# Another written-out order for the first thousand operations of an attention, MoE and bilinear kernel on one core

## The chip, the core and the metric

The kernel runs on one core of a Trainium2 chip. The core has four compute engines with a queue of instructions each: TensorE (PE in the profile; PEld is its weight load), VectorE (DVE), ScalarE (ACT) and GpSimd (POOL); SyncE (SP) issues most DMAs. Each engine works its own queue strictly in program order; between engines an instruction waits on semaphores. SBUF holds the tiles, PSUM the matmul results in banks of 128 partitions by 2 KB. The metric is the device time of one execution in microseconds (us), as the median of several runs.

## The reference

```python
scores = scale * q @ k^T                     # B 2, H 8, S 576, D 64
bias = -(cum[:, :, :, None] - cum[:, :, None, :])   # cum: running sum of max(s, 0)
scores = np.where(causal, -1e9, scores + np.minimum(bias, 0.0))
attn = softmax(scores); x = (attn @ v)       # x: 1152 x 512
logits = x @ w_gate; P = exp(logits - max)   # 8 experts, then 8 rounds of Sinkhorn
for e in range(E):
    h = np.maximum(x @ w1[e], 0.0)           # 512 -> 1024
    out += P[:, e:e+1] * (h @ w2[e])         # 1024 -> 512
a = x @ w_a; b = x @ w_b                     # x is out now; 512 -> 1536
return (a * b) @ w_out                       # 1536 -> 512
```

## The kernel before, in words

Every large product is made of three fp16 matmuls. Each fp32 operand is scaled by a power of two and split into a high and a low half; high times high, high times low and low times high are summed in PSUM. The power of two comes from the largest magnitude of the whole tensor, so before a weight can be used it has to be loaded, its squares' maxima taken (`w_prep`, L483; ACT at L521), reduced over a row (DVE, L451), reduced over the partitions, turned into a power of two (`pow2`, L257), and applied: ACT writes the high half (L296), DVE the low half (L310). The reduction over partitions is `all_max` (L472): a PE transpose (L477) into columns 320 to 456 of one of two PSUM banks, `xp0` and `xp1`, a DVE reduction (L478), and a PE matmul with ones (L479) that spreads the result. Those two banks are also where attention collects its output (L1161). `scales` (L620) does the same for q and k: L642 to L647, the matmuls L688 and L690, and a chain of small DVE steps, L653 to L674. `augs` (L697 to L706) uses its result for extra columns of k, which `k_prep` (L730) transposes by DMA (L753) into the tile `ka2`; q goes the same way through `q_prep` (L759).

The work is tiled by 128 tokens: 9 tiles, of which tile 8, the tail of both batches, is 64 rows of each. Tiles 0 and 4, the first of each batch, have only one block of keys and are done apart in fp32 (`first_tile`, L1093): transposes (L1125), scores (L1137), DVE maximum and subtraction (L1145, L1146), exponent on ACT (L1149), transpose (L1153), product with v (L1161). `x_tile` (L1168) normalizes a tile's output, transposes it (L1192) and splits it into `xt` (L1197 on ACT, L1199 on DVE). For the other tiles, `row_max` (L786; matmuls L799, mask L784, DVE L803), `shift` (L838; L846 to L848, PE L853) and `probs` (L862; scores L893 and L894, exponent L903, product with v L936 to L938) follow. The tail tile goes another way, `row_path` (L955), with 64-row matmuls at L998 and L1017.

The experts begin as soon as a tile of x and a unit of weights are there: `h_quad` (L1280) computes four blocks of 128 hidden units for 128 tokens into one PSUM bank, `mb0` or `mb1`, each as 12 matmuls of 128 columns (L1293 to L1295); ACT's Relu (L1299) and DVE (L1300) split it. I call 12 of these "12 h". `y_part` (L1304) multiplies by w2 (L1313 to L1315, 512 columns).

What sets the order: `Graph.add` collects every operation with its engine, its cost and the keys that it reads and writes. `schedule` then lays them out. For the operations before `cut` (1023 of them, up to the second expert) the order is written out in the table `ORDER`, whose entries are four times the operation's number plus the choice of engine; what lies behind the cut is laid out by a greedy list scheduler that starts from the times at which the table leaves the engines. `emit` (L165) issues the operations in that one sequence, so each engine's queue is the sequence's part for that engine. A dependency is tracked by the tile framework for whole tiles: a matmul into a PSUM bank waits for earlier readers of any column of that bank.

## Time and profile before

| | |
|---|---|
| median of 3 runs | 1007.16 us (1007.16 to 1007.33) |
| the profiled execution | 1006.66 us |
| its span, first to last instruction | 1004.9 us |
| PE busy | 986.5 us, 98% of the span |
| DVE busy | 784.2 us, 78% |
| ACT busy | 550.8 us, 55% |
| POOL busy | 101.1 us, 10% |
| granted PE clock | 1.00 by the page, in every stretch |

Times in the text are those of the profiled execution, counted from the start of its span. A row of the timeline gives the start, the duration of one piece (or of a run of like pieces, with their count), the engine, the line, the operation, what it writes and reads, and, if the engine stood idle before it, how long and what ended that. Matmuls are pipelined, so a matmul's duration is longer than its distance to the next one; the distance is what it costs.

### The profile page before, as it was taken

Reading aid. Unit: us, or ns where it says so; the run is one execution under the profiler, and the core shown is the slowest. Engines: PE = TensorE matmul, PEld = TensorE weight load, DVE = VectorE, ACT = ScalarE, POOL = GpSimd, SP = SyncE. Lnnn points to the kernel's source line nnn. Section 1 sums busy time; section 2 is a strip of 40 time slices with the busy share of each in tenths; the row PEclk is TensorE's granted clock in tenths of the full one; section 3 lists DMA queues with packets and bytes.
Section 4 is the critical chain, followed back from the end, with each engine's and each line's share of the span. In section 5 each row is a group of like instructions: output and inputs, shape, how many; then the busy total and the mean of one; then the engine's idle time right before and its main releaser. Section 6 shows DMA issues by size and latency. Waiting matters only on the chain.

```text
span 1004.9 us, 19286 instructions
## 1 busy us (share of the span) xinstructions
PE 986.5 (98%) x7714; PEld 636.3 (63%) x7714; DVE 784.2 (78%) x1688; ACT 550.8 (55%) x1062; POOL 101.1 (10%) x152
## 2 busy tenths in 40 slices
PE   6799999999999999999999999999999999999998
PEld 5677767776467447646744764674476464455777
DVE  4899986798867998885799888579988988676502
ACT  5898755457477347726634772663464455455220
POOL 3364554000000000000000000000000000000000
PEclk9999999999999999999999999999999999999999
DMA  9986999122133263233326323322636432322202
GB/s 232 212 163 126 172 160 173 34 84 85 45 104 105 84 220 133 77 113 109 105 84 224 132 75 114 107 105 84 226 138 253 108 84 84 126 85 85 84 22 74
DMA packets 152011, 121.40 MB, mean 121 GB/s; under 512 B 113361, under 2 KB 127697, under 8 KB 147313
## 3 DMA queue, kind: packets, MB, share of 16 engines
q1 hardware_dynamic: 147008, 117.78, 41.8%
q10 hardware_dynamic: 4912, 2.40, 1.0%
q8 instruction: 60, 0.98, 0.4%
q14 instruction: 31, 0.25, 0.1%
HBM read 79.26 MB, written 21.23 MB: 100 GB/s over the span
## 4 chain that ended last, share of the span: by engine, by line
PE 93%; DVE 3%; DMA 2%; ACT 1%; issue 1%; POOL 1%; ACTq 0%; DVEq 0%; POOLq 0%
PE yb L1313 10%; PE yb L1315 10%; PE yb L1314 10%; PE yb L1753 5%; PE yb L1755 5%; PE yb L1754 5%; PE mb L1753 4%; PE mb L1755 4%; PE mb L1754 4%; PE yb L2201 2%; PE yb L2200 2%; PE yb L2199 2%; PE mb L1313 2%; PE mb L1315 2%; PE mb L1314 2%; PE mb L2201 2%
## 5 line engine op out<-in xcount | busy, mean ns | idle before, releaser
L1315 PE MATMUL yb<-wun,ht 128*128 128x512 f16 x480 | 181.9, 379 | 0.0
L1314 PE MATMUL yb<-wun,ht 128*128 128x512 f16 x480 | 181.9, 379 | 0.0
L1313 PE MATMUL yb<-wun,ht 128*128 128x512 f16 x480 | 181.9, 379 | 0.0
L1315 PEld LDWEIGHTS <-ht 128*128 128x128 f16 x504 | 49.3, 98 | 59.5
L1313 PEld LDWEIGHTS <-ht 128*128 128x128 f16 x504 | 49.8, 99 | 57.8
L1314 PEld LDWEIGHTS <-ht 128*128 128x128 f16 x504 | 49.3, 98 | 57.8
L1753 PE MATMUL yb<-sx,wun 128*128 128x288 f16 x288 | 82.4, 286 | 0.0
L1754 PE MATMUL yb<-sx,wun 128*128 128x288 f16 x288 | 82.4, 286 | 0.0
L1755 PE MATMUL yb<-sx,wun 128*128 128x288 f16 x288 | 82.4, 286 | 0.0
L310 DVE SCALAR_TENSOR_TENSOR wun<-stage,sc,wun 128x1024 f16<-128x1024 f32 (+1 forms) x70 | 76.5, 1106 | 4.3 <-ACT wun L296 4.3
L1754 PEld LDWEIGHTS <-wun 128*128 128x128 f16 x672 | 65.7, 98 | 17.6 <-issue 0.4
L1753 PEld LDWEIGHTS <-wun 128*128 128x128 f16 x672 | 65.8, 98 | 17.3
L1755 PEld LDWEIGHTS <-wun 128*128 128x128 f16 x672 | 65.8, 98 | 16.6
L1936 DVE SCALAR_TENSOR_TENSOR acc<-yb,pe,acc 128x512 f32<-128x512 f32 x54 | 40.5, 750 | 38.6 <-PE yb L1315 38.4
L293 ACT ACTIVATE jk<-stage 128x1024 f16<-128x1024 f32 x52 | 54.7, 1053 | 26.9 <-DMA stage<-in_moe_w_dram 26.2
L296 ACT ACTIVATE wun<-stage,sc 128x1024 f16<-128x1024 f32 (+1 forms) x60 | 61.0, 1042 | 7.1 <-DVE sc L276 5.5
L296 ACT ACTIVATE wun<-h,sc 128x1024 f16<-128x1024 f32 x40 | 45.4, 1143 | 35.2 <-issue 13.8
L1753 PE MATMUL mb<-xt,wun 128*128 128x288 f16 x192 | 54.9, 286 | 0.0
L1755 PE MATMUL mb<-xt,wun 128*128 128x288 f16 x192 | 54.9, 286 | 0.0
L1754 PE MATMUL mb<-xt,wun 128*128 128x288 f16 x192 | 54.9, 286 | 0.0
L310 DVE SCALAR_TENSOR_TENSOR wun<-h,sc,wun 128x1024 f16<-128x1024 f32 x40 | 51.1, 1279 | 2.7 <-ACT wun L296 2.7
L1763 ACT ACTIVATE ht<-yb 128x288 f16<-128x288 f32 x96 | 38.9, 409 | 24.8 <-PE yb L1755 24.7
(585 smaller groups left out, 2654.2 us busy)
## 6 DMA issues: line engine op xcount, KB each, us to landing
stage<-in_moe_w_dram SPq DMA_DIRECT2D x26, 1024.0 KB, 5.1
md<-wun SPq DMA_DIRECT2D x18, 1024.0 KB, 4.0
wun<-md SPq DMA_DIRECT2D x12, 1024.0 KB, 4.9
mr<-in_moe_w_a_dram SPq DMA_DIRECT2D x12, 512.0 KB, 5.1
mr<-in_moe_w_b_dram SPq DMA_DIRECT2D x12, 512.0 KB, 4.3
mr<-in_moe_w_out_dram SPq DMA_DIRECT2D x12, 512.0 KB, 4.5
stage<-md SPq DMA_DIRECT2D x5, 1024.0 KB, 4.8
stage<-in_moe_w_dram SPq DMA_DIRECT2D x19, 256.0 KB, 3.5
```

The source lines that it names most:

```text
L293: nc.scalar.activation(out, src, AF.Square, accum_out=dst)
L296: nc.scalar.activation(hi, src, AF.Copy, scale=scale)
L310: eng.scalar_tensor_tensor(out=lo, in0=src, scalar=scale, in1=hi, op0=ALU.mult, op1=ALU.subtract)
L1313: nc.tensor.matmul(pp, lhsT=hh, rhs=wh, start=(f == 0), stop=False)
L1314: nc.tensor.matmul(pp, lhsT=hh, rhs=wl, start=False, stop=False)
L1315: nc.tensor.matmul(pp, lhsT=hl, rhs=wh, start=False, stop=(f == KF - 1))
L1753: nc.tensor.matmul(p, lhsT=wh, rhs=xh, start=first and ch == 0, stop=False, skip_group_check=True)
L1754: nc.tensor.matmul(p, lhsT=wh, rhs=xl, start=False, stop=False, skip_group_check=True)
L1755: nc.tensor.matmul(p, lhsT=wl, rhs=xh, start=False, stop=ch == 1, skip_group_check=True)
L1763: g.add("ACT", 52 + 120 + CN / 1.2, lambda: nc.scalar.activation(hh(), src(), AF.Relu), r=bk, w=k0, rank=-5)
L1936: g.add("DVE", 663, lambda t=t, z=z: nc.vector.scalar_tensor_tensor(out=acc[:, t], in0=yb[z], scalar=pe[:, t, e:e + 1], in1=acc[:, t], op0 ...
L2201: nc.tensor.matmul(p, lhsT=wl, rhs=xh, start=False, stop=ch == 1, skip_group_check=True)
```

## The change

Only the table changes. 42 lines of `ORDER` are replaced, that is the sequence of the 1023 operations before the cut; the engine chosen for each of them is the same as before. The new sequence comes from a search whose cost model also counts waits of a whole PSUM bank between its parts.

```diff
@@ -2483,48 +2483,48 @@
 SEL = (3, 5, 6, 7, 8)
 ORDER = (
     68, 145, 1508, 856, 0, 776, 20, 4, 72, 93, 8, 32, 96, 12, 76, 64, 16, 860, 41, 80, 180, 24, 36, 136,
-    292, 140, 177, 300, 173, 160, 44, 148, 48, 169, 196, 100, 296, 288, 304, 460, 188, 448, 156, 152, 432, 308, 192, 636,
+    292, 160, 44, 48, 140, 177, 300, 173, 148, 169, 100, 288, 460, 448, 432, 196, 304, 296, 308, 636, 456, 152, 156, 164,
...
```

Every compute engine's queue changes: of the operations before the cut, 284 stand elsewhere on PE, 231 on ACT, 277 on DVE and 101 on POOL. SP issues its DMAs in the same order as before. Behind the cut the same operations stand in almost the same sequence.

Three places matter most for what follows. The first is on PE, between tile 4's scores (L1137, into the banks `ss0` and `ss1`) and the maximum of w2 (L477, `xp0`). Before:

```order
L1137 MATMUL ss0_134<-pt2_110,pt3_111 128x128
L1137 MATMUL ss1_135<-pt2_110,pt3_111 128x128
L477 MATMUL xp0_138<-id32_60,sc_63 1x128
L479 MATMUL xp0_138<-sc_63,ones_61 128x1
L688 MATMUL xp0_138<-id32_60,sc_63 3x128
L690 MATMUL xp0_138<-sc_63,ones_61 128x3
L1293 LDWEIGHTS wun1_76
L1293 MATMUL mb1_85<-xt_71,wun1_76 128x128
```

and after:

```order
L1294 MATMUL mb1_85<-xt_71,wun1_76 128x128
L1295 LDWEIGHTS wun1_76
L1295 MATMUL mb1_85<-xt_71,wun1_76 128x128
L477 MATMUL xp0_138<-id32_60,sc_63 1x128
L479 MATMUL xp0_138<-sc_63,ones_61 128x1
L688 MATMUL xp0_138<-id32_60,sc_63 3x128
L1293 LDWEIGHTS wun1_76
L1293 MATMUL mb1_85<-xt_71,wun1_76 128x128
```

Ahead of the after rows, PE has 12 h (bank `mb1`) before the eight L1137, and 24 h (12 into `mb0`, 12 into `mb1`) between the last L1137 and L477; the last two rows ahead of L477 belong to these. Before, no h stood ahead of it. Another 12 h now stand between L688 and L690.

The second is DVE at the same place: tile 4's maxima and subtraction (L1145, L1146) against the reductions for w2 (L451, L478) and the scale of q and k (L642). Before:

```order
L1129 TENSOR_SCALAR pt3_111<-st0_136 128x512
L451 TENSOR_REDUCE sc_63<-sc_63 128x1
L478 TENSOR_REDUCE sc_63<-xp0_138 1x1
L1145 TENSOR_REDUCE mxr_124<-ss1_135 128x4
L287 TENSOR_REDUCE sc_63<-wgn_69 128x1
L642 TENSOR_REDUCE sc_63<-sc_63 128x2
L643 COPY sc_63<-sc_63 128x1
L266 TENSOR_SCALAR sc_63<-xp0_138 128x1
```

and after:

```order
L1129 TENSOR_SCALAR pt3_111<-st0_136 128x512
L1145 TENSOR_REDUCE mxr_124<-ss0_134 128x4
L1145 TENSOR_REDUCE mxr_124<-ss1_135 128x4
L451 TENSOR_REDUCE sc_63<-sc_63 128x1
L1146 TENSOR_TENSOR p32_1_107<-ss1_135,mxr_124 128x512
L478 TENSOR_REDUCE sc_63<-xp0_138 1x1
L287 TENSOR_REDUCE sc_63<-wgn_69 128x1
```

Both L1145 and one L1146 now stand ahead of L478, where before one L1145 stood behind it, the other further down and both L1146 behind L647.

The third is PE ahead of the first row_max matmul (L799), which reads the transposed keys `ka2`. Before:

```order
L1295 LDWEIGHTS wun1_76
L1295 MATMUL mb1_85<-xt_71,wun1_76 128x128
L1161 MATMUL xp0_138<-vf_133,pt0_108 128x65 x4
L1161 MATMUL xp1_139<-vf_133,pt1_109 128x65 x4
L799 LDWEIGHTS b3_0_102
L799 MATMUL ss1_135<-ka2_93,b3_0_102 128x256
```

and after:

```order
L1295 LDWEIGHTS wun0_75
L1295 MATMUL mb0_84<-xt_71,wun0_75 128x128
L1161 MATMUL xp1_139<-vf_133,pt1_109 128x65 x4
L1161 MATMUL xp0_138<-vf_133,pt0_108 128x65 x4
L1192 MATMUL st1_137<-id32_60,xb_113 128x128 x4
L479 MATMUL xp0_138<-sc_63,ones_61 128x1
L477 MATMUL xp1_139<-id32_60,sc_63 1x128
L799 LDWEIGHTS b3_0_102
L799 MATMUL ss1_135<-ka2_93,b3_0_102 128x256
```

L1192 (tile 4's x), the gate weights' L479 and the L477 for v of batch 0 moved ahead of the first L799; before, these stood some 50 rows behind it. The L451 that this last L477 reads stands on DVE 25 rows behind L706 in the new order.

Beside these: on ACT the first L521 square stands ahead of three stage loads (L499) instead of behind two of them; on DVE the first L451 of tile 0's scale stands ahead of w1's, and the copies L406 to L409 stand behind tile 0's L1199 instead of ahead of its L1176; both halves of tile 4's L1176 to L1181 stand ahead of the first L803. Of the tail tile's 64-row matmuls on PE there were 14 separate runs between other matmuls, and there are 10 now.

## Rows read from the trace of the kernel before

**Rows 1.** The page: busy us (share) xinstructions; shares of the chain by engine.

```profile
PE 986.5 (98%) x7714; PEld 636.3 (63%) x7714; DVE 784.2 (78%) x1688; ACT 550.8 (55%) x1062; POOL 101.1 (10%) x152
...
PE 93%; DVE 3%; DMA 2%; ACT 1%; issue 1%; POOL 1%; ACTq 0%; DVEq 0%; POOLq 0%
```

**Rows 2.** By stretch: us, busy of each engine (x), PEclk, DMA share, GB/s.

```profile
0.00:25.00 25.00, 16.27 (x86) 13.45 (x86) 11.92 (x42) 14.44 (x37) 8.04 (x21) 1.00 1.14 232
25.00:50.00 25.00, 19.68 (x168) 16.39 (x168) 20.44 (x64) 20.66 (x52) 9.20 (x15) 1.00 0.98 212
50.00:75.00 25.00, 24.59 (x316) 18.91 (x316) 23.56 (x66) 22.61 (x50) 14.86 (x18) 1.00 0.84 163
```

**Rows 3.** PE timeline: start, us, line, op, tiles, forms [idle before <-releaser].

```profile
31.37 2.08 PE L1137 MATMUL ss<-pt,pt 64*128 64x128 f32 x16 [0.78 <-DVE pt L1129]
34.23 0.37 PE L477 MATMUL xp<-id,sc 128*1 128x128 f32 x1 [0.77 <-DVE sc L451]
34.97 0.58 PE L479 MATMUL xp<-sc,ones 1*128 1x1 f32 x2 [0.37 <-DVE sc L478]
...
38.48 0.29 PE L1293 MATMUL mb<-xt,wun 128*128 128x128 f16 x1
```

**Rows 4.** PE timeline, h matmuls one after another at 43 us.

```profile
43.32 0.31 PE L1293 MATMUL mb<-xt,wun 128*128 128x128 f16 x1
43.43 0.27 PE L1294 MATMUL mb<-xt,wun 128*128 128x128 f16 x1
43.53 0.22 PE L1295 MATMUL mb<-xt,wun 128*128 128x128 f16 x1
43.59 0.22 PE L1293 MATMUL mb<-xt,wun 128*128 128x128 f16 x1
```

**Rows 5.** DVE timeline, chain of the maximum of w2.

```profile
34.01 0.16 DVE L451 TENSOR_REDUCE sc<-sc 128x1 f32<-128x8 f32 x1 [2.69 <-ACT wun L521]
...
36.29 0.15 DVE L271 TENSOR_SCALAR sc<-sc 128x1 f32<-128x1 f32 x1
...
41.78 0.27 DVE L674 TENSOR_SCALAR cst<-cst 128x1 f32<-128x1 f32 x1
...
44.10 0.21 DVE L706 TENSOR_TENSOR caug<-ctmp,caug 128x32 f16<-128x32 f32 x1
```

**Rows 6.** DVE timeline, first reduction of the weights.

```profile
16.10 0.16 DVE L451 TENSOR_REDUCE sc<-sc 128x1 f32<-128x8 f32 x1 [6.25 <-ACT wun L521]
```

**Rows 7.** PE timeline, first row_max (L799) and the first y.

```profile
50.46 0.27 PE L799 MATMUL ss<-ka,b 128*128 128x256 f16 x1
...
54.94 0.27 PE L477 MATMUL xp<-id,sc 128*1 128x128 f32 x1
55.05 0.60 PE L1192 MATMUL st<-id,xb 128*128 128x128 f32 x4
55.49 0.38 PE L1313 MATMUL mb<-wun,h 128*128 128x512 f16 x1
```

**Rows 8.** PE timeline, entry into a 64-row matmul.

```profile
146.98 0.38 PE L1315 MATMUL mb<-wun,h 128*128 128x512 f16 x1
147.29 0.62 PE L1017 MATMUL ss<-ka,b 128*64 128x512 f16 x4
```

**Rows 9.** DVE groups, 44.1 to 54 us: tiles, forms, count, busy us, mean ns.

```profile
L310 DVE SCALAR_TENSOR_TENSOR wun<-stage,sc,wun 128x512 f16<-128x512 f32 x6 | 5.0, 843 | 0.0
...
L1181 DVE TENSOR_TENSOR xb<-xp,rs 128x256 f32<-128x256 f32 x2 | 0.8, 424 | 0.1
...
L1300 DVE SCALAR_TENSOR_TENSOR h<-mb,h 128x512 f16<-128x512 f32 x1 | 0.7, 678 | 0.0
```

**Rows 10.** PE waits, 46 to 240 us: us in total, times, longest.

```profile
PE ss L799 <- DVE mxr L803: 0.4, 1, 0.4
PE mb L1315 <- DVE h L1300: 0.3, 1, 0.3
PE ss L1021 <- ACT p L1038: 0.2, 1, 0.2
```

## Prediction

> **What bounds the kernel now.** I read the page first: TensorE (PE) is busy 986.5 of 1004.9 us, and it makes up 93% of the chain that ended last [rows 1]. Only 18.4 us of the span are PE idle time, and the table by stretch says where: 25.00 − 16.27 = 8.7 us in the first 25 us and 25.00 − 19.68 = 5.3 us in the second, then 0.4 us in the third [rows 2]. The other 4 us are spread over the 930 us behind it and the end. The kernel is therefore bound by two things in turn: up to about 50 us by the latency of a chain over ScalarE (ACT), VectorE (DVE), PE and DMA, from there to the end by the amount of PE work. The change adds and removes no operation and changes none's engine, so PE's work stays as it is; only idle time, matmuls at the half clock and the cost of switching between kinds of matmul can change.

> The step that separates the two parts is the first row_max matmul (L799), at 50.46 us [rows 7]. Whatever PE has done by then is work that need not come later; whatever time it has lost by then is lost, unless idle time behind it can take it back, and there is hardly any: the waits of PE between 46 and 240 us are three, of 0.4, 0.3 and 0.2 us [rows 10]. So the first question is when L799 starts in the new order, and how much PE work stands ahead of it; the second is whether DVE, busy 23.56 of 25 us just then [rows 2], still delivers in time.

> **The change, part by part.** *The front, up to 30 us.* On ACT the first L521 square moves ahead of three L499 issues. Before, it stood behind two of them, the second of which waits for a stage buffer. On DVE the first L451 of scale 0 is no longer held: in the order before, w1's L451 stood ahead of tile 0's L1145 and ran at 16.10, after 6.25 us of idle that ACT's L521 ended [rows 6]. With that L451 and its square earlier by up to 1.1 us, the chain L477, L479, pow2, L310, L1161, L1192, L1199 comes earlier. Walked row by row with durations of before, L1199 gains about 0.6 us, since the L310s between are the same number on the same engine. PE idles there 8.7 us anyway, so nothing of this shows by itself. It is worth something only if the next part hands it on.

> *30 to 36 us: h ahead of the maximum of w2.* Before, PE ran tile 4's L1137 from 31.37, then w2's L477 at 34.23, as soon as DVE's L451 (34.01) had released it, and no h before 38.48 [rows 3, 5]. Now 12 h matmuls stand ahead of L1137 and 24 behind it, before L477. The first 12 fit: they wait for the cumc copies (L406 to L409, moved behind L1199) and run from about 30.05 to 31.35, in time that PE had idle. L1137 ends at about 33.4. The 24 then run at what h costs here, 43.43 − 43.32 = 0.11 us each at the lower of the two clock levels, 1.2 GHz (at 2.4 GHz it is 43.59 − 43.53 = 0.06) [rows 4]: 24 × 0.11 = 2.6, so L477 starts at 36.0 instead of 34.23, that is **+1.8 us** for w2's maximum. Behind it on PE stand L479 and L688; waiting for it are L478, pow2 (its L271 at 36.29 before), L647, L653 to L674 (41.78) and the augs (L706 at 44.10) [rows 5], then the DMA transposes of L753 that release L799. Part of the delay is given back: both L1145 and one L1146, which stood between these steps before, now run while DVE waits. By the walk L674 is 1.95 us late (before, one L310 stood behind it, now ahead) and L706 only 0.9.

> *Up to the first L799.* Two things hold it now. The transposes of L753 land some 1.0 to 1.3 us later than before. And v0's L477 now stands directly ahead of L799 on PE; it waits for v0's L451 on DVE, which stands 25 rows behind L706. Of these four are L310 (0.84 each), one is L1300 (0.68), two are L1181 (0.42) [rows 9], and some twenty are small, at 0.15 as L271 to 0.27 as L674 [rows 5], 3.1 together. The durations add to 3.4 + 0.7 + 0.8 + 3.1 = 8.0 us; one starts some 0.05 to 0.1 before the last has ended (L1300's neighbours too), which makes it about 6.7 for the 25 of them. From 45.2 that makes 51.9 to 53.2; I take 52.4, since most of these rows are queued back to back. L799 then starts at 52.8 us, **2.3 later**. Against that PE has already done what came later before: x4's L1192 (55.49 − 55.05 = 0.44), two L477 (0.11 each, 54.94 to 55.05) and one L479 (0.29, half of the 0.58 for two) [rows 3, 7], together 0.95. PE's net lag: 2.3 − 0.95 = **+1.3 us**, between +0.3 (only the transposes decide) and +2.0 (v0's L451 at the upper end).

> *L688 and L1161 behind whole banks.* L688 now follows DVE's L266, and L1161 DVE's L266 or L478, which read other columns of the same bank. By the walk these readers end before the matmul comes up or within 0.3 us of it, so I book 0. Should one be late by a whole reduction, a small one of 0.15 to 0.27 [rows 5], PE waits that long where it has idle time left before L799 in any case, and the cost is under 0.3; it can't gain.

> *From 55 us on.* The tail tile's L1017 and L998 (64-row matmuls) make PE switch: L1017 starts 147.29 − 146.98 = 0.31 us behind an ordinary y matmul [rows 8], where y follows y after 0.22, so a run costs about 0.09 on entry and at most as much on leaving. Such runs are 14 before and 10 in the new order: 4 × 0.09 to 4 × 0.2 = 0.4 to 0.8, I take **−0.6**. The three waits of 0.9 us [rows 10] belong to the old order; the new one has its own, which the trace can't show. Bounds: 0 and, if DVE's lag of 1 us meets PE at several gates, about 3 us; I take 0.9 again, hence 0. The part behind the cut has the same operations in nearly the same sequence: 0.

> **Sum.** +1.3 − 0.6 + 0 = +0.7 us against the profiled execution, 1006.66 (span 1004.9 and 1.76 around it). The median of the runs is 0.5 above that, so the forecast is 1007.16 + 0.7 = **1007.9 us**. Its own range runs from +0.3 − 0.8 − 0.9 = −1.4 (1005.8) to +2.0 + 2.1 − 0.4 = +3.7 (1010.9).

> **Rivals.** *Faster, 1005.0.* The 24 h run at the higher clock. In the trace the level rose at 43.43 [rows 4], within the run of h that began at 38.48 [rows 3]. If the 12 early h count and L1137 doesn't undo them, the 24 cost 24 × 0.05 = 1.2 us less and w2's L477 comes at 34.8, so PE's lag shrinks from 1.3 to 0.1; DVE's 0.6 us from the front then carries over too, the old waits of 0.9 go without new ones, and the switches give 0.8: +0.1 − 0.6 − 0.9 − 0.8 = −2.2. For it: h starts 8 us earlier (30.05 instead of 38.48). Against it: L1137, 2.08 us of dense fp32 matmuls from 31.37 [rows 3], was followed by h at the lower level, so this stretch before the 24 doesn't seem to help. It decides if the spacing of h is 0.06 already before 35 us. [...]

> *Slower, 1010.2.* DVE becomes the bound between 50 and 125 us. It is busy 23.56 of 25 us there [rows 2], so it can win back 1.4 us in a stretch at best. If it is 2 us late at the first L799, each L803, L848 and L1300 is, and PE, whose order is fixed, stands before L799, L853 and y. Price: lag 2.0, new waits of 3 instead of 0.9, and the switches give only 0.4 to 0.6: +2.0 + 2.1 − 0.5 = +3.6, less what overlaps, about 3.0. It decides where idle time of PE "released by DVE" adds to more than 2 us between 55 and 125 us.

> *No effect, 1007.2.* The front part moves only work inside idle time, and the whole bank waits held at the same places before; L799 starts within 0.3 us of its net old time, and the switches are made up for by other ones.

> **How the numbers follow.** A difference of 0.2%, 2.0 us, is about what a measurement of this kernel can tell from none: 1005.15 to 1009.17 is "the same". The forecast has 0.47, nearly all in that band; no effect 0.05; the faster rival 0.25; the slower one 0.23. Together: faster 0.25, same 0.51, slower 0.24 (the forecast's upper end adds a little to slower and takes from same). For 8 in 10 the range reaches a bit past each rival's price: 1004.0 to 1010.4.

> **What would show it.** Right: L799's first start near 52.8 with L1192 ahead of it, w2's L477 near 36.0, h at 0.11 spacing up to there, PE idle of about 14.4 + 1.3 = 15.7 us up to 75. Wrong: L799 before 51.5 (the lag is none), h at 0.06 spacing before 36 (the clock), or gaps of PE of over 0.5 us each between 55 and 125 us. If PE's busy time as a sum falls by more than 1 us, the clock or the switches were undersized; if it stays and idle falls, the front gave more than I granted it.

## The result, and the profile after

| | before | after |
|---|---|---|
| median of 6 runs | 1007.25 us (1006.81 to 1007.73) | 1015.9 us (1014.84 to 1017.64) |
| ratio | | 1.0086, 95% interval 1.0073 to 1.0099 |
| profiled execution, its span | 1006.66, 1004.9 us | 1016.7, 1015.0 us |

The change made the kernel slower by 8.7 us, where 1007.9 was forecast with a range of 1004.0 to 1010.4. Two lines of the page after, to be laid beside [rows 1]:

```profile
PE 988.2 (97%) x7714; PEld 635.9 (63%) x7714; DVE 796.6 (78%) x1688; ACT 550.9 (54%) x1062; POOL 101.3 (10%) x152
...
PE 84%; DVE 11%; issue 2%; ACT 2%; DMA 1%; POOL 1%; ACTq 0%; DVEq 0%; POOLq 0%
```

The span grew by 10.1 us: PE is busy 1.7 us longer with the same 7714 matmuls, and idle 8.4 us longer. DVE makes up 11% of the chain that ended last, where it had 3%. And DVE is busy 12.4 us longer with the same 1688 operations (796.6 against 784.2). The table by stretch says where PE's idle time lies (columns as in [rows 2]); after, from the start to 200 us:

```profile
0.00:25.00 25.00, 16.60 (x87) 13.61 (x88) 13.72 (x44) 15.10 (x38) 7.81 (x15) 1.00 1.13 230
25.00:50.00 25.00, 18.76 (x178) 15.70 (x177) 20.59 (x72) 20.95 (x54) 9.95 (x22) 1.00 0.94 217
50.00:75.00 25.00, 23.68 (x288) 17.47 (x289) 21.75 (x53) 18.89 (x42) 9.95 (x12) 0.86 0.63 124
75.00:100.00 25.00, 23.54 (x328) 17.80 (x326) 24.09 (x63) 19.21 (x39) 14.19 (x20) 1.00 0.84 126
100.00:125.00 25.00, 23.70 (x325) 18.13 (x324) 23.27 (x54) 19.70 (x37) 13.22 (x21) 1.00 1.00 163
125.00:150.00 25.00, 24.06 (x347) 18.10 (x345) 23.38 (x56) 14.85 (x25) 11.58 (x15) 1.00 0.97 156
150.00:175.00 25.00, 23.04 (x322) 14.46 (x320) 23.43 (x56) 13.66 (x23) 16.44 (x17) 1.00 0.97 167
```

and the last of these stretches before:

```profile
150.00:175.00 25.00, 25.00 (x475) 18.03 (x474) 16.41 (x42) 13.26 (x24) 10.18 (x10) 1.00 1.05 162
```

Against [rows 2], the first two stretches nearly balance (0.3 us less idle, then 0.9 more). The third has 0.9 more idle time and a granted clock of 0.86 instead of 1.00. From 75 to 175 us PE is idle for 1.46 + 1.30 + 0.94 + 1.96 = 5.7 us, where the old order had 0.55. With the 1.75 us of the third place below, these differences make up the 8.4 us: 0.6 up to 50 us, 0.9 to 75, 5.1 to 175 and 1.75 behind it. (PEclk, the column with the granted clock, does not show the half clock of the start: in both kernels it has 1.00 where h still follows h at 0.11 us, up to 30.8 us after and up to 43.4 before.) And DVE, which in the old order is through with most of its attention work by 150 us (16.41 busy of 25), is at 23.4 of 25 until 175. The waits of PE after, from 46 to 240 us (columns: us in total, times, longest), to be laid beside [rows 10]:

```profile
PE xp L477 <- DVE sc L451: 2.1, 1, 2.1
PE yb L1270 <- DVE logit L1250: 1.7, 1, 1.7
PE st L1192 <- DVE xb L1181: 1.7, 1, 1.7
PE ss L853 <- DVE ut L848: 1.3, 1, 1.3
PE st L1017 <- ACT p L1038: 1.2, 1, 1.2
PE mb L1313 <- DVE h L1300: 0.8, 1, 0.8
```

**First place: ahead of the first L799.** The timeline of PE after:

```profile
30.78 0.31 PE L1295 MATMUL mb<-xt,wun 128*128 128x128 f16 x1
31.03 2.07 PE L1137 MATMUL ss<-pt,pt 64*128 64x128 f32 x16
33.03 0.23 PE L1293 MATMUL mb<-xt,wun 128*128 128x128 f16 x1
...
34.27 0.22 PE L1294 MATMUL mb<-xt,wun 128*128 128x128 f16 x1
34.33 0.22 PE L1295 MATMUL mb<-xt,wun 128*128 128x128 f16 x1
34.55 0.27 PE L477 MATMUL xp<-id,sc 128*1 128x128 f32 x1
...
47.97 0.65 PE L1192 MATMUL st<-id,xb 128*128 128x128 f32 x4 [1.67 <-DVE xb L1181]
...
50.99 0.37 PE L477 MATMUL xp<-id,sc 128*1 128x128 f32 x1 [2.06 <-DVE sc L451]
51.16 0.42 PE L799 MATMUL ss<-ka,b 128*128 128x256 f16 x1
...
52.44 0.63 PE L1313 MATMUL mb<-wun,h 128*128 128x512 f16 x1
52.86 0.63 PE L1314 MATMUL mb<-wun,h 128*128 128x512 f16 x1
```

The h behind L1137 follow one another at 34.33 − 34.27 = 0.06 us, where those ahead of it had 0.11: the clock is at its higher level before 35 us, and w2's L477 starts at 34.55 instead of the 36.0 forecast. But PE, now ahead with its work, stands idle 1.67 us for L1192 and 2.06 us for v0's L477, and there the clock falls to its half again (PEclk is 1.00 from 48 to 50 us and 0.51 from 50 to 52): y follows y at 52.86 − 52.44 = 0.42 us, twice the 0.22 of the kernel before. (As an estimate from longer runs of y, 512 columns in 0.427 and in 0.215 us make 1.2 and 2.4 columns per ns; that is what the traces show of the two levels which the prediction and e3's expectation give as 1.2 and 2.4 GHz.) The eight matmuls from 51.16 to 52.44 take 1.28 us (0.66 before), and the 12 of y, to 57.22, take 4.8 (2.6 before). Together 2.8 us.

**Second place: DVE from 80 to 175 us.** The timeline of DVE after, around 150 us:

```profile
142.89 1.50 DVE L979 TENSOR_TENSOR pt<-p,pt 128x384 f16<-128x384 f32 x1 [0.46 <-POOL pt L977]
...
146.16 1.29 DVE L976 CAST pt<-p 128x512 f16<-128x512 f32 x1
...
149.56 0.68 DVE L1025 TENSOR_REDUCE mxr<-ss 128x1 f32<-128x512 f32 x1
...
150.40 1.56 DVE L979 TENSOR_TENSOR pt<-p,pt 128x512 f16<-128x512 f32 x1
```

GpSimd in the same stretch:

```profile
142.82 1.16 POOL L980 TENSOR_TENSOR pt<-p,pt 128x512 f16<-128x512 f32 x1
...
146.01 1.16 POOL L980 TENSOR_TENSOR pt<-p,pt 128x512 f16<-128x512 f32 x1
...
149.57 0.61 POOL L977 CAST pt<-p 128x512 f16<-128x512 f32 x1 [0.87 <-ACT p L1038]
150.26 1.15 POOL L980 TENSOR_TENSOR pt<-p,pt 128x512 f16<-128x512 f32 x1
```

And ScalarE, a little later:

```profile
154.11 0.78 ACT L1038 ACTIVATE p<-st,nbi,cst 128x512 f32<-128x512 f32 x1 [1.40 <-DVE nbi L1028]
```

Three DVE operations that start while a GpSimd L980 runs end 0.3 to 0.6 us after L980's end and last two to three times as long as the shortest of their kind (1.50, 1.29 and 1.56 us against 0.55, 0.41 and 0.68); L1025, which reads PSUM, has its ordinary 0.68 us beside L977. The lateness then goes to ACT's L1038, which waits 1.40 us for DVE's L1028, and to PE's L1017, which waits 1.19 us for L1038. The groups of DVE from 50 to 175 us (columns as in [rows 9]) say the same, after:

```profile
L979 DVE TENSOR_TENSOR pt<-p,pt 128x384 f16<-128x384 f32 x4 | 3.9, 975 | 0.5 <-POOL pt L977 0.5
L1027 DVE TENSOR_TENSOR mxr<-mxr,mx 128x1 f32<-128x1 f32 x8 | 3.7, 457 | 0.3
```

and before:

```profile
L979 DVE TENSOR_TENSOR pt<-p,pt 128x384 f16<-128x384 f32 x4 | 2.2, 554 | 0.0
L1027 DVE TENSOR_TENSOR mxr<-mxr,mx 128x1 f32<-128x1 f32 x8 | 2.1, 258 | 0.3
```

I counted over the whole trace the DVE operations that took over 0.15 us longer than the shortest of the same line and size: 22 with 8.3 us of excess before, 35 with 17.7 us after, and every one of them, in both kernels, overlaps a GpSimd operation. I call this sum the stretched time; its growth is 9.4 of the 12.4 us by which DVE is busy longer. The stretched operations, with two operands or with one (L976 above, a cast), read SBUF alone, and they end 0.01 to 0.6 us after the GpSimd operation's end, the short ones at once (L1027, on one column, after 0.01 to 0.02) and the long ones later (L310, on 512 columns, after 0.53 to 0.55, in the kernel after). Of the 67 DVE operations after that read PSUM and start beside a GpSimd operation, none took over 0.09 us longer than the shortest of its line and size. By what mechanism, no run shows.

**Third place: the seam at the cut.** The first matmul behind the cut, L1270, writes the bank `yb` and waits 1.75 us (203 to 205 us) for DVE's L1250, the read of the last gate logits, which lay in `xp`; the two tiles share PSUM space, one after the other. In the old order L1250 stands ahead of the x sums (L1635); in the new order it stands behind all the L1635 of the table and starts at 204.81 us.

### The profile page after: what moved, and what is told of

Read it like the earlier page. It is cut to its first block, busy times and chain, and to the rows that moved or that the text cites. A ratio compares the mean times of both kernels' runs of the same rounds, so it can differ in the third digit from the quotient of the medians.

```text
span 1015.0 us, 19294 instructions
## 1 busy us (share of the span) xinstructions
PE 988.2 (97%) x7714; PEld 635.9 (63%) x7714; DVE 796.6 (78%) x1688; ACT 550.9 (54%) x1062; POOL 101.3 (10%) x152
## 4 chain that ended last, share of the span: by engine, by line
PE 84%; DVE 11%; issue 2%; ACT 2%; DMA 1%; POOL 1%; ACTq 0%; DVEq 0%; POOLq 0%
PE yb L1313 10%; PE yb L1315 10%; PE yb L1314 10%; PE yb L1755 5%; PE yb L1754 5%; PE yb L1753 5%; PE mb L1753 3%; PE mb L1754 3%; PE mb L1755 3%; PE yb L2201 2%; PE yb L2200 2%; PE yb L2199 2%; PE mb L2201 2%; PE mb L2200 2%; PE mb L2199 2%
## 5 line engine op out<-in xcount | busy, mean ns | idle before, releaser
L1315 PE MATMUL yb<-wun,ht 128*128 128x512 f16 x480 | 181.9, 379 | 0.0
L1313 PE MATMUL yb<-wun,ht 128*128 128x512 f16 x480 | 181.9, 379 | 0.0
L1315 PEld LDWEIGHTS <-ht 128*128 128x128 f16 x504 | 49.3, 98 | 59.5
L1313 PEld LDWEIGHTS <-ht 128*128 128x128 f16 x504 | 49.9, 99 | 57.5
L310 DVE SCALAR_TENSOR_TENSOR wun<-stage,sc,wun 128x1024 f16<-128x1024 f32 (+1 forms) x70 | 78.3, 1129 | 2.1 <-ACT wun L296 2.1
L1754 PEld LDWEIGHTS <-wun 128*128 128x128 f16 x672 | 65.8, 98 | 17.7 <-issue 0.2
L1755 PEld LDWEIGHTS <-wun 128*128 128x128 f16 x672 | 65.7, 98 | 16.6
L296 ACT ACTIVATE wun<-h,sc 128x1024 f16<-128x1024 f32 x40 | 45.5, 1144 | 34.7 <-DVE h L1566 13.3
L310 DVE SCALAR_TENSOR_TENSOR wun<-h,sc,wun 128x1024 f16<-128x1024 f32 x40 | 51.0, 1279 | 2.8 <-ACT wun L296 2.7
```

Of the source, the lines that this page charges most:

```text
L296: nc.scalar.activation(hi, src, AF.Copy, scale=scale)
L310: eng.scalar_tensor_tensor(out=lo, in0=src, scalar=scale, in1=hi, op0=ALU.mult, op1=ALU.subtract)
L1313: nc.tensor.matmul(pp, lhsT=hh, rhs=wh, start=(f == 0), stop=False)
L1315: nc.tensor.matmul(pp, lhsT=hl, rhs=wh, start=False, stop=(f == KF - 1))
L1754: nc.tensor.matmul(p, lhsT=wh, rhs=xl, start=False, stop=False, skip_group_check=True)
L1755: nc.tensor.matmul(p, lhsT=wl, rhs=xh, start=False, stop=ch == 1, skip_group_check=True)
```

## The experiments

Each ratio is to the kernel before, measured on the same chip at the same time. "Less GpSimd work" means that GpSimd writes 16 columns only of those low halves of the softmax weights that it makes, in L980 for tiles 5 to 8 (the row path is taken by these four, not by the tail tile alone); the rest of them is left out. Theory 1 puts the loss on the clock ahead of L799, theory 2 on VectorE beside GpSimd in the rest of the order; later ones add the seam.

| run | median us | ratio, 95% interval | stretched DVE time, us |
|---|---|---|---|
| e1 new order to the first L799, old behind | 1009.5 | 1.0029 (1.0018 to 1.0041) | 10.9 |
| e2 old to the first L799, new behind | 1018.05 | 1.0111 (1.0096 to 1.0126) | 17.8 |
| e3 after, PE kept busy ahead of L799 | 1014.49 | 1.0081 (1.0055 to 1.0107) | 16.7 |
| e4 after, less GpSimd work (L980) | 1014.18 | 1.0075 (1.0055 to 1.0096) | 11.5 |
| e5 before, less GpSimd work (L980) | 1006.29 | 0.9985 (0.9976 to 0.9995) | 7.0 |
| e6 after, old sequence behind the cut | 1016.56 | 1.0087 (1.0072 to 1.0102) | 16.6 |
| e7 e3, e4 and e6 together | 1013.6 | 1.0069 (1.0044 to 1.0095) | 11.5 |
| e8 before, extra GpSimd work | 1065.88 | 1.0583 (1.0567 to 1.0599) | 19.9 |
| e9 after, gate read earlier | 1016.04 | 1.0082 (1.0061 to 1.0103) | 19.4 |
| e10 new to tile 5's row path, old behind | 1013.26 | 1.0055 (1.0035 to 1.0075) | 11.0 |
| e11 old to tile 5's row path, new behind | 1012.66 | 1.0055 (1.0036 to 1.0073) | 13.3 |
| e12 e3 and e9 together | 1016.98 | 1.0089 (1.0062 to 1.0116) | 18.7 |
| e13 e11, less GpSimd work (L980) | 1010.13 | 1.0028 (1.0016 to 1.0040) | 6.6 |
| e14 e13, gate read earlier | 1008.66 | 1.0015 (1.0004 to 1.0026) | 6.1 |
| e15 e10, PE kept busy ahead of L799 | 1012.16 | 1.0043 (1.0028 to 1.0057) | 15.4 |
| e16 e15, less GpSimd work (L918, L980) | 1010.12 | 1.0021 (1.0008 to 1.0035) | 8.4 |
| e17 after with all of these | 1011.27 | 1.0034 (1.0022 to 1.0047) | 7.6 |

Single executions of the kernels with the new front differ by 4 us and more (e17: 1008.35 to 1013.0). In part that goes with the clock. In the profile after, it falls at 50 us; in those of e9, e10, e12, e15 and e16 it falls at 43 to 45 us, ahead of the two gaps, behind a wait of 1.6 to 1.9 us for ScalarE's L1149. In e9 h follows h at 0.06 us up to 44.4 us and at 0.11 from 44.6. In e16 the four executions whose mean granted clock is 1.000 took 1005.85 to 1009.88 us, the six others 1009.73 to 1011.94. The clock is not all of it: two executions of e12 with 1.000 took 1013.04 and 1018.02. So the verdicts below rest on the waits of the profiles as much as on the medians.

### Which part of the order (e1, e2, e10, e11)

The table is cut at one operation: all that stands ahead of it in one order, then the rest in the sequence of the other.

```diff
 ORDER = (
-    (the new table)
+    (the new table up to the first L799), (the rest as in the old table)
...
-        self.schedule(self.cut, None, state)
+        self.schedule(self.cut, None, state, POST)
```

`POST` is the sequence behind the cut, written out, of the kernel whose table the end comes from. e2 takes the old table first, e10 and e11 cut ahead of the first operation of tile 5's row path, at about 105 us.

> The new order up to and including the first row_max matmul (L799), the old order behind it and behind the cut. Theory 1 (the clock: PE stands idle ahead of the first L799 and runs the first y at half rate): most of the loss is here, 1010 to 1012 us. Theory 2 (the part behind L799 loses the time, because VectorE operations that run beside GpSimd operations take longer there): only what the half rate costs, under 3 us and partly recovered, 1007 to 1009.5 us, and the stretched VectorE time falls back towards the 8 us of the kernel before. Whichever holds, y at 0.43 us spacing from 51 to 57 us should be seen again.

> The old order up to and including the first L799, the new order behind it and behind the cut. Theory 1 (clock): the idle time ahead of L799 is gone, so no half rate and about 1007 to 1008.5 us. Theory 2 (VectorE beside GpSimd, behind L799): 1012 us or more, with waits of PE that VectorE and ScalarE end, as in the changed kernel, between 80 and 210 us.

e1 gave 1009.5, the front alone 0.29%; e2 gave 1018.05. So the order behind L799 loses by itself more than the whole change (1.0111 against 1.0086), and most of the loss lies there, as theory 2 had it. The prediction of e2 by theory 1 failed, and one line of its profile shows why the two don't simply add: x4's L1192, which the new order does right behind the first L799, waits 1.97 us there, and the clock falls in this kernel too (PEclk 0.93 from 50 to 75 us).

> The new order up to the first operation of tile 5's row path (585 operations, to about 105 us), the old one behind it and behind the cut. The front alone gave 1009.5. If the middle (tiles 1 to 3) loses time by itself, through L853 behind VectorE operations stretched by GpSimd (1.4 us) and smaller ones: 1011 to 1012.5. If the lag is only handed on and the loss is made in the row path: 1009 to 1010.

> The old order up to the first operation of tile 5's row path, the new one behind it. The wait at the first L1270 (1.75 us) belongs to it in any case: 1009. If L980 beside L979 and L1027 stretches VectorE here without any lag brought along, the waits at L1017 and L1313 (1.2 + 0.6 + 0.8) come on top: 1011 to 1012. If those waits only arise from arriving late: 1008.5 to 1009.5.

Both halves lose as much on their own, 1.0055 each, and together more than the whole; e10 has in it the front, which costs 0.29% alone. e10 is above what I expected, e11 a little above what the second theory gave. e11 is the cleanest of all, since its first 100 us are those of the kernel before (75 to 100 us: PE 25.00), and yet its waits from there on are those of the changed kernel:

```profile
PE yb L1270 <- DVE logit L1250: 1.7, 1, 1.7
PE st L1017 <- ACT p L1038: 1.2, 1, 1.2
...
PE mb L1313 <- DVE h L1300: 0.8, 1, 0.8
```

They do not come from arriving late; this part of the order makes them.

### The clock (e3, e15)

```diff
+    def keep_busy(n):
+        for _ in range(n):
+            nc.tensor.matmul(ss[0][:, 0:128], lhsT=idb, rhs=idb, start=True, stop=True)
...
+    g.pre = {191: lambda: keep_busy(28), 228: lambda: keep_busy(32)}
```

191 and 228 are L1192 of tile 4 and the L477 of v0; `emit` calls `pre` ahead of these operations.

> The changed kernel with 28 extra matmuls of 128 columns ahead of x4's L1192 and 32 ahead of v0's L477, into a score bank that nothing reads, in the two stretches of 1.7 and 2.1 us in which PE waits for VectorE. Theory 1: the clock stays at 2.4 GHz, the first y group runs at 0.22 us spacing, and the time falls by the 2.7 us that the half rate costs or more, to 1013 us or below. Theory 2: the first y group is faster as well, but PE then waits longer behind it: 1014 to 1016 us. If the clock falls nevertheless, the y rows stay at 0.43.

The extra matmuls lie where PE was idle (line numbers of this kernel are 3 higher):

```profile
45.87 1.73 PE L2417 MATMUL ss<-idb 128*128 128x128 bf16 x28
...
50.36 0.27 PE L802 MATMUL ss<-ka,b 128*128 128x256 f16 x1
...
51.02 0.38 PE L1316 MATMUL mb<-wun,h 128*128 128x512 f16 x1
51.23 0.38 PE L1317 MATMUL mb<-wun,h 128*128 128x512 f16 x1
```

The clock stays up, y follows y at 0.21 us, and the first y group is done at 53.6 instead of 57.2 us. Of these 3.6 us 1.4 are left at the end, within what the medians scatter by: the waits behind take the rest back. The clock's fall is real; alone it doesn't decide.

> The order of the run that is new up to tile 5's row path (1013.3), with 60 extra matmuls ahead of the first L799 that keep PE busy. If the half clock behind that idle time is worth what it lasts (2 to 2.7 us) and isn't given back: 1010.5 to 1011.5. If the waits behind it (L853 1.3, L1315 1.5) take it back: 1012.5 to 1013.5.

1012.16 against 1013.26, between the two expectations, and not told apart by the intervals. L853 waits 1.7 us here, 1.3 without the extra matmuls. But this profile doesn't show what a clock that stays up is worth, for it fell all the same:

```profile
25.00:50.00 25.00, 21.55 (x191) 19.00 (x191) 19.15 (x64) 21.45 (x55) 10.18 (x22) 0.86 0.94 216
```

It fell at 43 us, before the extra matmuls began, and at the half clock the first 28 of them took 2.8 us instead of 1.7. Of the eight executions the three with a mean granted clock of 1.000 took 1010.1 to 1011.14 us, about the first expectation; the other five reach from 1009.73 to 1014.41. So what the clock costs at the end of the kernel is open here: between nothing and some 3 us.

### VectorE beside GpSimd (e4, e5, e8, e13, e16)

```diff
-                lambda: nc.gpsimd.tensor_tensor(out=lo, in0=src, in1=hi, op=ALU.subtract)),
+                lambda: nc.gpsimd.tensor_tensor(out=lo[:, 0:16], in0=src[:, 0:16], in1=hi[:, 0:16], op=ALU.subtract)),
```

> The changed kernel, with GpSimd writing 16 instead of 256 to 512 columns in the low halves of the softmax weights of tiles 5 to 8 (L980, 18 operations of about 1.15 us); the rest of those low halves is left as it was. Theory 1: nothing but GpSimd's own time goes, 1015 us within 1. Theory 2: the VectorE operations beside L980 are no longer stretched (17.7 us of extra time should fall by about 10), the waits at 121, 139, 153 and 170 us shrink, and the time falls by 3 to 5 us, to 1010.5 to 1013.

> The kernel before with the same part left out as in the run before this one (GpSimd's low halves of tiles 5 to 8 on 16 columns only). If stretched VectorE time costs only where VectorE is late, the old order gains little: its three waits of 0.9 us are all that could go, so 1006 to 1007 us. If GpSimd's share costs both orders alike, it gains 2 us as well, to about 1005.

e4 gave 1014.18, which lies in the range of theory 1 (1014 to 1016) and not of theory 2, with stretched time down by 6.2 us; its L1017 and L1313 no longer wait by more than 0.3 us, but L1052 waits 1.8 for a DMA transpose in their place. The old order gained 0.15% from the same omission (e5), and the new one no more, 0.11% (1.0086 to 1.0075). With this work left out of both, the new order is as far behind as before, within the scatter. These two runs, then, show no price of L980 for the change as a whole.

> The order of the run that is new from tile 5's row path on (1012.7), with GpSimd's low halves of tiles 5 to 8 (L980) on 16 columns; the rest of them is left as it was. If the stretched VectorE time (13.3 us there, 8.3 before) makes the waits at L1017 and L1313: they go, and 1009.5 to 1010.5, of which 1.75 are the gate's. If the order waits anyway (for DMA transposes or ScalarE): 1011.5 or more.

1010.13, in the range of the theory: from 1.0055 to 1.0028 with stretched time from 13.3 to 6.6 us. Of these 0.27% the old order gains 0.15% too (e5), so about 0.12% belong to the new order; and 0.28% are left with less stretched time than the kernel before has (8.3 us), so the sum of it is not a measure of the loss. The waits of e13:

```profile
PE yb L1270 <- DVE logit L1250: 1.7, 1, 1.7
...
PE xp L1052 <- DMA raw<-pt: 0.7, 1, 0.7
...
PE mb L1313 <- DVE h L1300: 0.2, 1, 0.2
```

L1017's 1.2 us are gone and L1313's 0.8 are 0.2; the seam's 1.7 is the largest, then come 0.9 at L1293 (for DVE's L310), 0.8 at L479 and the DMA wait. In e16 tile 2's low halves (L918) also leave GpSimd, as plain copies on ScalarE:

```diff
-                lambda hi=hi, lo=lo, src=src: nc.gpsimd.tensor_tensor(out=lo, in0=src, in1=hi, op=ALU.subtract)),
+                (lambda lo=lo, src=src: nc.scalar.activation(lo, src, AF.Copy)) if t == 2 else ...
```

> As the run before, with GpSimd's low halves of tile 2 (L918) written by ScalarE as plain copies and those of tiles 3 and 5 to 8 on 16 columns, so that L654, L586 and L587 (1.7 us stretched ahead of L848) should be stretched less. If they make the wait at L853: it falls from 1.3 to 0.5 or less, and the time by 1 to 2 us against the run before. If not, the same time as that run.

Before this, in e15, the largest of the waits reads

```profile
PE ss L856 <- DVE ut L851: 1.9, 2, 1.7
```

and in e16 all that is left behind 46 us is

```profile
PE xp L941 <- DVE pt L920: 0.3, 1, 0.3
PE st L896 <- ACT p L906: 0.3, 1, 0.3
```

The wait of L853 (L856 here) is gone and the median 2.0 us lower; up to 1.5 of that may be the L980 of tiles 5 to 8, left out here too, which gained e5 0.15%. In the changed kernel L654 lasted 0.94 us, L586 1.00 and L587 0.55, each beside a GpSimd operation, ahead of the L848 for which L853 waits; in e16 the same three have 0.17, 0.16 and 0.14, and in e17, where the clock stays up and the wait is gone as well, the same. Stretched VectorE time made that wait. What is left of e16's loss is not waiting behind 46 us; it goes in part with the clock (above).

> The kernel before with 122 extra GpSimd operations (differences of 256 columns, into a tile that nobody reads there) in three bursts behind its partition reductions at 231, 254 and 380 us, where GpSimd is idle, PE 100% and VectorE above 80% busy. Nobody waits for them. Theory 2: VectorE operations with two operands in SBUF that run beside them take 0.3 to 0.6 us longer, VectorE's stretched time rises from 8 us to 20 or more, and since it has little slack there PE waits, 3 to 15 us slower. Without such contention: VectorE's durations stay and the time is 1007.

```diff
+    def pool_work(n):
+        scr = big["ab"]
+        a = id32.rearrange("p (o k) -> p o k", o=1).to_broadcast([128, 2, 128])
+        for _ in range(n):
+            nc.gpsimd.tensor_tensor(out=scr.rearrange("p (o k) -> p o k", o=2), in0=a, in1=a, op=ALU.subtract)
```

The stretched time rose from 8.3 to 19.9 us, about as theory 2 had it (20 or more). The 58 us of loss, though, are not its price. The timeline of GpSimd in this kernel has the first burst and the reduction behind it:

```profile
240.12 28.63 POOL L2419 TENSOR_TENSOR ab<-id 128x256 f32<-128x256 f32 x32 [7.15 <-issue]
274.56 0.38 POOL L461 PARTITION_ALL_REDUCE sc<-sc  x1 [5.81 <-issue]
```

The burst started 7 us late and each operation took 0.9 us, so the next reduction came at 274.56 instead of 254.27, and PE waited 14.5 and 17.4 us for what hangs on it, and 17.6 us behind the last burst. The experiment shows the stretching and not its cost.

### The seam (e6, e9, e14)

> The changed kernel with the operations behind the cut in the sequence that they have in the kernel before (written out). The wait of the gate matmul L1270 for VectorE's L1250 at 203 us (1.75 us) is there in every run with the new sequence behind the cut and in none with the old. If it is a cause of its own, the time falls by 1.5 to 1.9 us, to about 1014; if VectorE's lag only moves it, the wait comes back elsewhere before 300 us and the time stays near 1015.9.

The wait stayed, 1.7 us, at the same place, and the time did not move: the sequence behind the cut is not its cause. L1250 belongs to the part ahead of it. So e9 moves one entry of the table:

```diff
 ORDER = (
...
+    (L1250 and L1251, directly behind their matmul)
...
-    (L1250 and L1251, behind the x sums)
```

> The changed kernel with one VectorE operation moved back: the read of the last gate logits (L1250, L1251) directly behind its matmul, ahead of the x sums (L1635), as in the kernel before. Theory (the first matmul behind the cut, L1270, writes a bank that the gate logits lay in, and waits for L1250 behind 8 L1635): the wait of 1.75 us at 203 us goes, nothing else changes, 1014.1 within 0.7. If L1270 then waits for something else as long: 1015.9.

> As the run before, and the read of the gate logits (L1250) moved back directly behind its matmul. If the two causes make up the whole loss of this half: 1007.5 to 1008.5. If the gate's wait is only replaced: the same as the run before.

In e9's profile the stretch from 200 to 300 us, with 98.25 us of PE busy after, has

```profile
200.00:300.00 100.00, 100.00 (x643) 62.88 (x642) 81.79 (x170) 57.25 (x103) 1.21 (x2) 1.00 0.21 69
```

so the wait is gone. The median is unmoved at 1016.04, short of the expected 1014.1; in its profiled execution the half clock lasted longer (up to 58 us from its fall at 44.4, against 57 from 50.0 in that of the changed kernel), and the four runs reach from 1013.77 to 1016.48, so the median can't tell. In e14, where the front is the old one, it does: 1008.66 against 1010.13, 1.5 us of the 1.75 (a little above the expected 1008.5), and the second half of the order is within 0.15% of the kernel before, or 0.30% behind e5, which leaves out the same GpSimd work. L1052 waits 1.6 us for a DMA transpose there, 0.7 in e13: some of the gain is taken back.

### Together (e7, e12, e17)

> The changed kernel with all three: PE kept busy ahead of the first L799 (60 extra matmuls), GpSimd's low halves of tiles 5 to 8 on 16 columns, and the old sequence behind the cut. If the three are the causes, the sum of their gains (1.4, 1.7 and 1.8 us, and the second more where the first no longer hides it) brings it to 1009 to 1011 us; the rest would be the remaining waits between 75 and 135 us. If the waits merely move, 1013 or more.

> The changed kernel with PE kept busy ahead of the first L799 and the read of the gate logits moved back. If the two gains add (1.4 and 1.75 us): 1012.7. If the gate's wait is only reached earlier with PE busy, still 1014.5.

> The changed kernel with PE kept busy ahead of the first L799 (60 extra matmuls), the gate read (L1250) directly behind its matmul, GpSimd's low halves of tile 2 written by ScalarE as plain copies and those of tiles 5 to 8 on 16 columns. The new order to the row path gave 1010.1 with its part of these, the new order from there 1008.7 with its part. If the causes are these and add: 1010 to 1012 (the rest of both, 3 and 1.5 us above before). If the waits move on to others: 1013.5 or more, as with the three that left tile 2 and the gate as they were.

e7 came out worse than I had added up, where I had put "the waits merely move": the seam is still in it, L853 untouched, L1052 waits 2.6 us for DMA transposes. In its profile and in that of e12 the clock had fallen before the extra matmuls, as in e15. e12 shows no gain; its four runs reach from 1013.04 to 1018.02. e17, with all of them, gave 1011.27, as the sum of the two halves had it: of 8.7 us 4.1 are left, some 5 against e5, which also has less GpSimd work. The largest waits left in its profile are

```profile
PE xp L1055 <- DMA raw<-pt: 2.9, 4, 1.0
PE xp L480 <- DVE sc L454: 0.9, 1, 0.9
```

that is L1052, which waits four times for the transposes of its weights, and v0's L477. The DMA waits stand where the DVE waits stood: the new order puts the row path's product with v (three of the four waits are of tiles 5 to 7, one of the tail tile) close behind what it needs. Whether these four and the scatter of the clock make up the whole remainder is open. No version of the new order beats the kernel before.

## Why the prediction was wrong

- **What bounds the kernel.** Right that the first 50 us are a chain and that PE's work is unchanged. Wrong that from there on PE's work alone sets the end: DVE stood at 91 to 94% from 50 to 150 us in the kernel before already, and what kept PE fed was the place of each DVE operation, not the sum.
- **The front.** L1199 came 0.8 us earlier (27.90 against 28.74), as walked (0.6). The 24 h did not cost 2.6 us: they ran at the higher clock, at 0.06 us each, so w2's L477 came 0.3 us late and not 1.8, L706 0.25 us early (43.85 against 44.10) and not 0.9 late, and v0's L451 at 50.79 and not 52.4 (6.7 us behind the end of L706, the lower bound of my walk). L799 started 0.7 us late instead of 2.3; with the 0.95 us of work done ahead, PE was 0.25 us early where I had +1.3. My argument that L1137 would leave the clock low was wrong. PE's idle time up to 75 us came out at 16.0 us, where 15.7 was to show that I was right: that is chance, since all three signs of being wrong came true as well (L799 before 51.5, h at 0.06 before 36, gaps of 1.3 and 0.6 us between 55 and 125) and the idle time lies elsewhere.
- **The step that failed there** is the one that followed: I named the h at the higher clock as the faster rival, and its deciding point (0.06 us spacing before 35 us) came true, but not its time. PE's earlier work bought idle time of 1.67 and 2.06 us ahead of L799, and the half clock behind it cost 2.8 us in the profiled execution. My sum had nothing for it: I had looked for the rise of the clock and not for its fall.
- **L688 and L1161.** Booked at 0, and right: 0.25 us of idle time at L688, none at L1161. But the whole bank wait that counted was at the seam, 1.75 us at L1270. "The part behind the cut: 0" was wrong, since the table also sets when the last reads of the attention's banks end.
- **New waits from 55 us on.** The term I put at 0.9, with 3 as its upper end, measured 5.7 us of idle time between 75 and 175 us and 1.75 at the seam. This is the term that broke the range. I bounded it by PE's waits of before, which only tell how well the old order fits. Of the 5.7 us the runs trace 3.3 to stretched DVE operations (L853 1.3, L1017 1.2, L1313 0.8); for the other waits, of 0.2 to 0.6 us each, no run shows the cause. The effect stood in the trace of before: 22 DVE operations stretched beside GpSimd, L1251 among them with 1.19 us for an operation of 0.3. I took DVE durations from the rows as if they were an operation's own.
- **The slower rival** (1010.2) had the right engine, the right place and the right sign: idle time of PE put down to DVE or what hangs on it passed its 2 us. Its price was too small, since it had DVE late by a fixed 2 us, where the new order kept adding to it.
- **Switches.** Fewer runs of 64-row matmuls were to give 0.6 us; no run separates it, and PE's busy time shows none of it. It rose by 1.7 us: the half clock behind L799 adds 2.8, and the h that ran at 0.11 us (41 before, 12 after) take 29 × 0.05 = 1.5 off, which makes 1.3 without any gain.

## What to carry to other kernels

An order that a search has fitted to fixed durations can lose where durations depend on what runs beside them, as those of VectorE did here (8.3 us stretched before, 17.7 after): before moving VectorE and GpSimd work against each other, list the operations that lasted longer than the shortest of their kind and see what overlapped. When an experiment leaves work out, leave it out of the kernel before as well, and compare with that. Ask of matmuls brought forward where the engine will stand idle for it: here PE then waited 1.67 and 2.06 us ahead of the next step, and the clock that fell there cost 2.8 us in the profiled execution. And a change that ends at a seam is judged by the first waits behind the seam too: which bank does the next stage reuse, and who reads it last.
